# Attention with the softmax numerators of two steps in one tile: the second pair of heads of a step shares a tile with the first pair of the next

## The chip, the cores and the metric

The kernel runs on one core of one Trainium2 chip. The metric is device time in microseconds (us), the median of several runs. Engines are named as in the profile: PE is TensorE (matmuls), PEld its weight loads, ACT is ScalarE, DVE is VectorE, POOL is GpSimd, SP is SyncE, which issues most DMAs.

## The reference

One transformer block on 2048 tokens of width 448: adaptive layer norm (shift, scale and gate come from a condition `c`), attention with 16 heads of 28, a second adaptive layer norm, and an MLP of width 1792.

```python
mod = (_silu(c) @ w_mod).reshape(c.shape[0], 6, 1, -1)          # sa, ca, ga, sb, cb, gb
h = _layernorm(x) * (1 + ca) + sa
q, k, v = split(h @ wqkv)                                        # 16 heads of 28
p = softmax(q @ k.T * 28 ** -0.5)                                # per head, 2048 x 2048
x = x + ga * ((p @ v) @ wo)
h = _layernorm(x) * (1 + cb) + sb
x = x + gb * (_gelu(_layernorm(h) @ w1 + b1) @ w2 + b2)
```

All is float32. Matmuls take float32 operands as two rounded parts, a high and a low one (`hi`, `lo`), and sum three products of them.

## The kernel before

The kernel has three stages. Up to about 181 us it loads and splits weights, normalises, and computes Q, K and V; Q and K are parked in HBM by groups of four heads. From there to about 850 us it computes attention. The rest is the MLP.

**Attention** is a loop of 256 steps, 16 units of 16 steps. A unit is one group `g` of four heads and one block `qt` of 512 queries; a step takes one tile `kt` of 128 keys. The program is written in the order in which it runs, and each engine takes its instructions in that order. A step does the following.

- *Scores.* For each pair of heads (`hf` 0, then 1) PE writes a PSUM tile `s` of 128 keys x 2 heads x 512 queries: three products (hi hi, lo hi, hi lo) per head, so six matmuls of 32 rows a pair (L1046). Heads 0 and 1 use the array's rows 0 to 63, heads 2 and 3 the rows 64 to 127. `s` has two buffers, so the first pair's scores of a step wait until the first Exp of the step before has read its buffer, and the second pair's for the second Exp. From about step 236 on it has three.
- *Exp.* Behind each pair, ScalarE takes `exp(SCALE * s)` into the tile `pt` (L1051): two heads of 512 queries, 1024 elements a partition. The **first Exp** of a step is that of heads 0 and 1, the **second Exp** that of heads 2 and 3. The softmax maxima are in the scores already (they enter as an extra row of Q), and the sums come out of the product with V through a column of ones.
- *Maxima of later units.* Between the score matmuls, `emit_max` inserts three or four small jobs a step, in turns: PE computes a block of approximate scores into a PSUM tile `mx` of three buffers (L392), and VectorE reduces it to its maximum (L397). They use the half of the array that the scores beside them leave free. They last until about step 236.
- *P times V ("AV").* PE multiplies V with the Exps of the step **before** (`pend`, L1054): four matmuls, one a head, each in 32 columns of the array (L1016). In the profile each is two records, so 8 a step. They use all 128 rows of the array, so the scores of the next step stand behind them.

At a unit's end ScalarE copies the output tile `o` to `osb` (L984), and over the next steps it is divided by its sums and stored or, in the last four units (one per query block), multiplied with `wo` (steps 8 to 11 of a unit).

**Where P lies.** `pt` is a tile of four heads, 128 x 4 x 512, in one of three places of SBUF, `c0`, `c1` and `d0`, in turns (`ptags`, L1021 and L1035): a step's four heads are one tile. The profile calls them `slot_c` and `slot_d`. In stage one the places hold other data. A tile laid in a place must wait for the last that was there: for its readers (AV, on PE) and for its writers (Exps, on ScalarE). The first instruction that writes into it carries these waits. The tile framework puts them there, one semaphore per engine waited for; a wait on PE for scores and one for AV are one wait, for the later of the two. The wait for an earlier writer on ScalarE is a second one.

**An instruction and its waits.** Where an instruction needs two waits, the built program has an instruction in front of it that does nothing but wait; the profile calls it EVENT_SEMAPHORE.

Of the kernel before, what the change touches and what calls it, by code (L numbers as in the profile page):

```python
# [13 lines left out]
F32 = mybir.dt.float32  # L14
F32R = mybir.dt.float32r
AF = mybir.ActivationFunctionType
# [21 lines left out]
SCALE = float(DH) ** -0.5  # L38
# [3 lines left out]
def tile_adaln_block(ctx: ExitStack, tc: tile.TileContext, x, wqkv, wo, w1, b1, w2, b2, c, w_mod, out):  # L42
    nc = tc.nc
    pe, act, dve, pool, sp = nc.tensor, nc.scalar, nc.vector, nc.gpsimd, nc.sync
# [11 lines left out]
    def nm(t):  # L56
        uid[0] += 1
        return f"{t}_{uid[0]}"
# [4 lines left out]
    def slot(tag, shape, dt=F32R):  # L63
        return sb.tile(shape, dt, tag="slot_" + tag, name=nm("slot_" + tag), bufs=1)
# [11 lines left out]
    def ps_s2():  # L76
        return psp[0].tile([128, 2, 512], F32, tag="s", name=nm("s"), bufs=psp[2])
# [7 lines left out]
    def ps_o():  # L85
        return o_pool[0].tile([128, 512], F32, tag="o", name=nm("o"), bufs=1)
# [183 lines left out]
    d0 = slot("d0", [128, 4, 512], F32)  # L270
# [30 lines left out]
    v_sb = [sb.tile([128, 4, H, 32], F32, tag=f"slot_v{i}", name=f"v{i}", bufs=1) for i in range(4)]  # L301
# [141 lines left out]
    def tick_late(force=False):  # L443
        for e in late:
            e[0] -= 1
        while late and late[0][2] in qst and (force or late[0][0] <= 0):
            late.pop(0)[1]()
# [44 lines left out]
    def emit_max(n, half=None):  # L492
        for _ in range(n):
            if not mxq:
                return
            fits = [x for x, m in enumerate(mxq[:32]) if half is None or (m[4] // 2 == half and m[4] != last_j[0])]
            g, qt, cch, i, j = mxq.pop(fits[0] if fits else 0)
            last_j[0] = j
            max_one(g, qt, cch, i, j)
            count(g, qt, [cch])  # L500
# [27 lines left out]
    def finish_max(g, qt):  # L528
        while left[(g, qt)] > 0:
            emit_max(1)  # L530
# [42 lines left out]
    def load_k(g, ch):  # L573
        kst[(g, ch)] = load_parts(f"a{ch}", 1, g, slice(ch * 512, (ch + 1) * 512))

    def load_q(u):
        g, qt = divmod(u, NB)
        qst[u] = load_parts(f"b{u % 2}", 0, g, slice(qt * 512, (qt + 1) * 512))
# [107 lines left out]
    def share(n_mx, n_s):  # L686
        if shared:
            shared.pop().__exit__(None, None, None)
        shared.append(tc.tile_pool(name=nm("ps"), bufs=1, space=PSUM))
        psp[:] = [shared[0].__enter__(), n_mx, n_s]  # L690
# [291 lines left out]
    def end_unit(u, o):  # L982
        o_sb = sbt("osb", [128, 512], bufs=2)
        act.copy(o_sb, o)  # L984
        base = (u + 1) * NKT
        for d, fn in unit_end_tasks(u, o_sb):
            at(base + 1 + d, fn)

    pend = None
    o = None  # L990
# [14 lines left out]
    def n_maxima(s_):  # L1005
        n_plain, n_wo = left_steps(s_)
        over = len(mxq) - 7 * n_plain // 2
        if is_wo(s_):
            return max(0, -(-over // max(n_wo, 1))) if s_ % NKT > 8 else 0
        plain[0] += 1  # L1010
        return 4 if plain[0] % 2 or (over > 3 * n_wo and over > 0) else 3

    def av(u, kt, p, o):
        g = u // NB
        for j in range(4):
            pe.matmul(  # L1016
                o[32 * j : 32 * j + 32, :], v_sb[kt // 4][:, kt % 4, 4 * g + j, :], p[:, j, :],
                start=(kt == 0), stop=(kt == NKT - 1),
            )

    ptags = ["c0", "c1", "d0"]  # L1021
    done_max = set()
    for u in range(NU):
        g, qt = divmod(u, NB)
        for kt in range(NKT):
            step = u * NKT + kt
            if kt == 1 and u + 1 < NU and u + 1 not in qst:
                load_q(u + 1)
            if kt == NKT - 6 and u + 1 < NU:
                finish_max(*divmod(u + 1, NB))  # L1030
            tick_late()
            if not (three or mxq or late):
                three = True
                share(1, 3)
            pt = slot(ptags[step % 3], [128, 4, 512], F32)  # L1035
            n = n_maxima(step)
            n0 = 1 if n == 3 and step % 4 == 3 else 2

            ks, qs = kst[(g, kt // 4)], qst[u]
            kc = slice((kt % 4) * 128, (kt % 4 + 1) * 128)  # L1040
            for hf in range(2):
                s2 = ps_s2()
                for term, (kp, qp) in enumerate(((0, 0), (1, 0), (0, 1))):
                    for jj in range(2):
                        rows_ = slice(64 * hf + 32 * jj, 64 * hf + 32 * jj + 32)
                        pe.matmul(s2[:, jj, :], ks[rows_, kp, kc], qs[rows_, qp, :], start=(term == 0), stop=(term == 2))  # L1046
                    if hf == 0 and term < min(n0, n):
                        emit_max(1, 1)
                    if hf == 1 and ((term == 0 and n - n0 > 0) or (term == 2 and n - n0 > 1)):
                        emit_max(1, 0)  # L1050
                act.activation(pt[:, 2 * hf : 2 * hf + 2, :], s2, AF.Exp, scale=SCALE)  # L1051
            if pend is not None:
                pu, pkt, pp, po = pend
                av(pu, pkt, pp, po)  # L1054
                if pkt == NKT - 1:
                    end_unit(pu, po)
            if kt == 0:
                o = ps_o()
            pend = (u, kt, pt, o)
            if qt == NB - 1 and kt % 4 == 3 and g + 1 < NG:  # L1060
                load_k(g + 1, kt // 4)
            for fn in sched.pop(step, ()):
                fn()
    av(*pend)
    end_unit(pend[0], pend[3])
    tail = {}
# [87 lines left out]
```

## Time and profile before

| | us |
|---|---|
| median of 3 runs | 1149.93 |
| lowest and highest | 1149.39 and 1150.04 |
| the profiled execution, first to last instruction (its span) | 1147.0 |
| attention, first to last AV, in the profile | 185.2 to 851.8 |

The time of a run is a little longer than the span of a profiled one, since it also holds what lies before the first and behind the last instruction: 2.9 us, if the profiled execution took the median.

How the rows of the profile are read: in a timeline a row is the start, the length, engine, line of the kernel, operation, written tile <- read tiles, shapes, how many instructions were merged into it, and in brackets how long the engine was idle before it and what is thought to have ended that. In a group the figures are total busy time and the mean in ns of one. The end of a matmul is modelled, and matmuls in different rows or columns of the array run at the same time, so a busy PE may still have room. TensorE's granted clock was 1.000 over the whole span.

### The profile page before, as it was taken

What the parts mean: (1) busy time and instruction counts of PE and PEld (TensorE: products, weight loads), DVE (VectorE), ACT (ScalarE), POOL (GpSimd) and SP (SyncE); (2) the same over time, 40 slices, a digit from 0 to 9 for tenths busy, and PEclk for the clock granted to TensorE, in tenths of its full rate; (3) what the DMA queues carried; (4) which work ended last, traced back from release to release, by engine and by line L of the source; (5) the groups of instructions that cost most, each with busy time, mean ns of one, the idle gap of its engine ahead of it and who ended that gap; (6) DMA issues with size and microseconds to landing.
All of it is one profiled execution on the core that took longest, in us unless ns stands there. A gap on an engine that the chain in (4) does not pass through costs nothing.

```text
span 1147.0 us, 20808 instructions
## 1 busy us (share of the span) xinstructions
PE 1134.5 (99%) x8380; PEld 679.5 (59%) x8380; DVE 828.7 (72%) x1487; ACT 682.5 (60%) x839; POOL 216.8 (19%) x235
## 2 busy tenths in 40 slices
PE   8999999999999999999999999999999999999998
PEld 6767765444443444444444444545458888888887
DVE  6868788999998899989999977583648853444322
ACT  4656757777777877777877777675862321111110
POOL 2534432210000000000000011204514503123000
PEclk9999999999999999999999999999999999999999
DMA  9642354111132111321110222022213100000000
GB/s 299 204 148 110 107 184 130 44 60 57 45 96 66 57 39 38 94 66 57 59 55 21 83 84 62 24 84 68 68 46 95 42 33 1 1 33 1 33 1 33
DMA packets 51305, 81.09 MB, mean 71 GB/s; under 512 B 12700, under 2 KB 21760, under 8 KB 51208
## 3 DMA queue, kind: packets, MB, share of 16 engines
q1 hardware_dynamic: 50248, 78.73, 21.6%
q8 instruction: 66, 1.08, 0.4%
q0 software_dynamic: 672, 0.56, 0.2%
q10 hardware_dynamic: 288, 0.46, 0.1%
q14 instruction: 31, 0.25, 0.1%
HBM read 53.11 MB, written 26.35 MB: 69 GB/s over the span
## 4 chain that ended last, share of the span: by engine, by line
PE 96%; DVE 1%; ACT 1%; issue 1%; SPq 0%; DMA 0%; DVEq 0%; POOL 0%; POOLq 0%; ACTq 0%
PE s L1046 27%; PE o L1016 22%; PE mx L317 16%; PE pa L339 7%; PE mx L392 6%; PE s L1104 4%; PE s L1105 4%; PE s L1103 4%; PE pa L317 3%; PE pa L276 1%; PE o L240 1%; PE mx L240 1%; ACT slot_c L1051 0%; PE o L547 0%; PE pa L279 0%
## 5 line engine op out<-in xcount | busy, mean ns | idle before, releaser
L397 DVE TENSOR_REDUCE mxp<-mx 128x1 f32<-128x512 f32 x919 | 579.6, 685 | 105.9 <-PE mx L392 101.2
L1046 PE MATMUL s<-slot_b,slot_a 32*128 32x512 f32 x3072 | 383.7, 422 | 1.9 <-ACT full L814 0.7
L1051 ACT ACTIVATE slot_c<-s 128x1024 f32<-128x1024 f32 x342 | 331.6, 1022 | 83.8 <-PE s L1046 82.3
L1046 PEld LDWEIGHTS s<-slot_b,slot_a 32*128 32x128 f32 x3072 | 214.4, 183 | 254.5 <-ACT slot_c L1051 151.3
L392 PE MATMUL mx<-kh,qh 32*128 32x512 f32 x899 | 289.6, 470 | 1.2 <-DVE mxp L397 0.9
L1051 ACT ACTIVATE slot_d<-s 128x1024 f32<-128x1024 f32 x170 | 164.8, 1021 | 42.7 <-PE s L1046 42.6
L1016 PE MATMUL o<-slot_c,v 128*32 128x512 f32 x1368 | 183.1, 605 | 0.6 <-ACT osb L984 0.4
L1087 ACT ACTIVATE full<-mx,b_col 128x512 f32<-128x512 f32 x56 | 38.6, 689 | 191.8 <-PE mx L317 175.3
L392 PEld LDWEIGHTS mx<-kh,qh 32*128 32x128 f32 x899 | 116.1, 182 | 8.5 <-DVE mxp L397 5.2
L1090 DVE CAST hi<-full 128x512 fp32r<-128x512 f32 x56 | 25.2, 451 | 129.2 <-ACT full L1087 129.2
L783 POOL TENSOR_TENSOR osb<-osb,osb 128x512 f32<-128x512 f32 x16 | 20.9, 1305 | 463.4 <-DMA osb<-drec 295.1
L1016 PE MATMUL o<-slot_d,v 128*32 128x512 f32 x680 | 90.6, 605 | 0.0
L1016 PEld LDWEIGHTS o<-slot_c,v 128*32 128x32 f32 x1368 | 27.1, 108 | 57.5 <-issue 53.7
L317 PE MATMUL mx<-y,slot_a 128*128 128x512 f32 x160 | 60.6, 395 | 0.0
L405 ACT ACTIVATE slot_d<-mx 128x512 f32<-128x512 f32 x48 | 27.0, 596 | 40.1 <-PE mx L392 40.0
L1091 DVE TENSOR_TENSOR lo<-full,hi 128x512 fp32r<-128x512 f32 x56 | 44.1, 788 | 5.2
L317 PE MATMUL mx<-y,slot_c 128*128 128x512 f32 x152 | 47.5, 396 | 0.1
L1105 PE MATMUL s<-slot_v,lo 128*128 128x448 f32 x128 | 46.7, 365 | 0.0
L1103 PE MATMUL s<-slot_v,hi 128*128 128x448 f32 x128 | 46.6, 364 | 0.0
L317 PE MATMUL mx<-y,slot_v 128*128 128x512 f32 x112 | 39.2, 396 | 0.0
L317 PE MATMUL mx<-y,slot_b 128*128 128x512 f32 x112 | 39.1, 398 | 0.0
L339 PE MATMUL pa<-slot_c,slot_a 128*128 128x512 f32 x136 | 37.0, 405 | 0.0
(223 smaller groups left out, 1388.7 us busy)
## 6 DMA issues: line engine op xcount, KB each, us to landing
d<-lo SPq DMA_DIRECT2D x32, 256.0 KB
slot_b<-d SPq DMA_DIRECT2D x32, 256.0 KB
slot_a<-d SPq DMA_DIRECT2D x32, 256.0 KB
d<-hi SPq DMA_DIRECT2D x20, 256.0 KB
osb<-drec SPq DMA_DIRECT2D x14, 256.0 KB
out_dram<-xn SPq DMA_DIRECT2D x16, 224.0 KB
slot_v<-in_w_mod_dram SPq DMA_DIRECT2D x4, 784.0 KB
raw<-in_B_w_dram SPq DMA_DIRECT2D x14, 224.0 KB
```

Source lines behind the costliest of these rows:

```text
L317: pe.matmul(p, a, b, start=(i == 0), stop=(i == len(terms) - 1))
L339: pe.matmul(p, *ts[i], start=(i == 0), stop=(i == len(ts) - 1))
L392: pe.matmul(m, qh_sb[(g, qt)][js, i * 128 : (i + 1) * 128], k[js, :], start=True, stop=True)
L397: dve.tensor_reduce(out=mxp[(g, qt)][:, i, j, cch : cch + 1], in_=m, op=ALU.max, axis=AX.X)
L1016: pe.matmul(o[32 * j : 32 * j + 32, :], v_sb[kt // 4][:, kt % 4, 4 * g + j, :], p[:, j, :], start=(kt == 0), stop=(kt == NKT - 1),)
L1046: pe.matmul(s2[:, jj, :], ks[rows_, kp, kc], qs[rows_, qp, :], start=(term == 0), stop=(term == 2))
L1051: act.activation(pt[:, 2 * hf : 2 * hf + 2, :], s2, AF.Exp, scale=SCALE)
L1087: act.activation(gf, p, AF.Gelu_apprx_tanh, bias=b1_col[:, i : i + 1])
L1091: dve.tensor_tensor(out=glo, in0=gf, in1=f(ghi), op=ALU.subtract)
L1103: pe.matmul(pp, ghi[:, ts], w_hi, start=(m == 0), stop=False)
L1104: pe.matmul(pp, ghi[:, ts], w_lo, start=False, stop=False)
L1105: pe.matmul(pp, glo[:, ts], w_hi, start=False, stop=(m == NFT - 1))
```

## The change

A tile of P still holds four heads in one of the same three places, but it begins half a step later. A step's first Exp writes into the second half of the tile that the step before began (`p_next[:, 2:4, :]`); its second Exp lays a new tile and writes into its first half, and the next step's first Exp fills that one up. `pt` becomes a list of two halves, and AV reads heads 0 and 1 from one tile and heads 2 and 3 from the next. The first half of the pattern is primed by a tile laid before the loop, in `c1`.

```diff
             pe.matmul(
-                o[32 * j : 32 * j + 32, :], v_sb[kt // 4][:, kt % 4, 4 * g + j, :], p[:, j, :],
+                o[32 * j : 32 * j + 32, :], v_sb[kt // 4][:, kt % 4, 4 * g + j, :], p[j // 2][:, j % 2, :],
...
-    ptags = ["c0", "c1", "d0"]
+    p_no = [0]
+
+    def p_tile():
+        p_no[0] += 1
+        return slot(("c0", "c1", "d0")[p_no[0] % 3], [128, 4, 512], F32)
+
+    p_next = p_tile()
...
-            pt = slot(ptags[step % 3], [128, 4, 512], F32)
+            pt = [p_next[:, 2:4, :]]
...
-                act.activation(pt[:, 2 * hf : 2 * hf + 2, :], s2, AF.Exp, scale=SCALE)
+                if hf == 1:
+                    p_next = p_tile()
+                    pt.append(p_next[:, 0:2, :])
+                act.activation(pt[hf], s2, AF.Exp, scale=SCALE)
```

No instruction of an engine is added, removed or passed by another. What moves are the tiles, and with them the waits. On ScalarE, three consecutive steps of the first unit before the change (the written tile, the scores read, and the semaphores waited for; the two Exps of a step stand one below the other, and the scores `s_2324` and `s_2338` are one step's):

```order
L1051 ACTIVATE slot_c_545_2282<-s_2283 128x1024 [waits PE_49,Activation_49]
L1051 ACTIVATE slot_c_545_2282<-s_2297 128x1024 [waits PE_49]
L1051 ACTIVATE slot_d_554_2323<-s_2324 128x1024 [waits PE_49,Activation_49]
L1051 ACTIVATE slot_d_554_2323<-s_2338 128x1024 [waits PE_49]
L1051 ACTIVATE slot_c_560_2353<-s_2354 128x1024 [waits PE_49,Activation_49]
L1051 ACTIVATE slot_c_560_2353<-s_2368 128x1024 [waits PE_49]
```

The same three steps after it:

```order
L1060 ACTIVATE slot_d_545_2277<-s_2283 128x1024 [waits PE_49]
L1060 ACTIVATE slot_c_552_2310<-s_2297 128x1024 [waits PE_49,Activation_49]
L1060 ACTIVATE slot_c_552_2310<-s_2324 128x1024 [waits PE_49]
L1060 ACTIVATE slot_c_560_2348<-s_2338 128x1024 [waits PE_49,Activation_49]
L1060 ACTIVATE slot_c_560_2348<-s_2354 128x1024 [waits PE_49]
L1060 ACTIVATE slot_d_567_2381<-s_2368 128x1024 [waits PE_49,Activation_49]
```

The wait for an earlier Exp (`Activation_49`) stood at a step's first Exp and stands at its second one. Counted over the program, first Exps with two or more waits are 251 of 256 before and 2 after; second Exps with two are none before and 252 after.

On PE, the second pair of scores of a step of the same unit, an AV and the first scores behind it, before (`o` is the output, `v` is V):

```order
L1046 MATMUL s_2623<-slot_b_429_1795,slot_a_494_2048 128x512 [waits Activation_49]
L1046 MATMUL s_2623<-slot_b_429_1795,slot_a_494_2048 128x512
L392 MATMUL mx_2626<-kh_294_1276,qh_283_1235 128x512 [waits DVE_49]
L1046 MATMUL s_2623<-slot_b_429_1795,slot_a_494_2048 128x512 x4
L1016 MATMUL o_2176<-slot_c_606_2571,v_258 32x512 [waits Pool_49]
L1016 MATMUL o_2176<-slot_c_606_2571,v_258 32x512 x3
L1046 MATMUL s_2639<-slot_b_429_1795,slot_a_494_2048 128x512 [waits Activation_49]
```

And after:

```order
L1052 MATMUL s_2623<-slot_b_429_1795,slot_a_494_2048 128x512 [waits Activation_49]
L1052 MATMUL s_2623<-slot_b_429_1795,slot_a_494_2048 128x512
L392 MATMUL mx_2626<-kh_294_1276,qh_283_1235 128x512 [waits DVE_49]
L1052 MATMUL s_2623<-slot_b_429_1795,slot_a_494_2048 128x512 x4
L1016 MATMUL o_2177<-slot_c_606_2566,v_258 32x512 [waits Pool_49]
L1016 MATMUL o_2177<-slot_c_606_2566,v_258 32x512
L1016 MATMUL o_2177<-slot_d_613_2599,v_258 32x512 x2
L1052 MATMUL s_2639<-slot_b_429_1795,slot_a_494_2048 128x512 [waits Activation_49]
```

AV takes two matmuls from each of two tiles; its only wait here is the one for V, which it had before.

## The prediction

> **What bounds the kernel now.** I read the page first, for the share of each engine and the chain that ended last.
>
> ```profile
> span 1147.0 us, 20808 instructions
> PE 1134.5 (99%) x8380; PEld 679.5 (59%) x8380; DVE 828.7 (72%) x1487; ACT 682.5 (60%) x839; POOL 216.8 (19%) x235
> ...
> PE 96%; DVE 1%; ACT 1%; issue 1%; SPq 0%; DMA 0%; DVEq 0%; POOL 0%; POOLq 0%; ACTq 0%
> ```
>
> By these, TensorE is the limit and ScalarE matters nowhere. But a score matmul uses half of the array's rows, so a busy PE can still be waiting with its other half. So I asked the trace for the Exp line (L1051): its instructions, what ScalarE idled for before them (indented, us and times), and who waited for them.
>
> ```profile
> L1051 ACTq EVENT_SEMAPHORE  x251: 17/17/1592, 180.7 to 849.3; - x126
> ...
>   PE s L1046: 124.9, 245
> ...
>   PEld s L1046: 225.7, 334
> ```
>
> ScalarE waited 245 times for scores, and the weight loads of scores waited 334 times for an Exp: the two engines pass work in a ring. There is also an instruction that only waits for a semaphore, 251 times in 256 steps.
>
> Third, the timeline of two steps in the middle, per engine. The first column is the start in us, the second the length of the merged piece, the last the idle time before it. Weight loads of PE:
>
> ```profile
> 438.17 0.16 PEld L1016 LDWEIGHTS o<-slot_d,v 128*32 128x32 f32 x8 [0.29 <-issue]
> 439.17 0.18 PEld L1046 LDWEIGHTS s<-slot_b,slot_a 32*128 32x128 f32 x2 [0.84 <-ACT slot_c L1051]
> ...
> 440.33 0.16 PEld L1016 LDWEIGHTS o<-slot_c,v 128*32 128x32 f32 x8 [0.37 <-issue]
> 441.33 0.18 PEld L1046 LDWEIGHTS s<-slot_b,slot_a 32*128 32x128 f32 x2 [0.84 <-ACT slot_c L1051]
> ...
> 442.22 0.19 PEld L1046 LDWEIGHTS s<-slot_b,slot_a 32*128 32x128 f32 x2 [0.36 <-ACT slot_c L1051]
> ...
> 443.12 0.16 PEld L1016 LDWEIGHTS o<-slot_c,v 128*32 128x32 f32 x8 [0.28 <-issue]
> 444.11 0.18 PEld L1046 LDWEIGHTS s<-slot_b,slot_a 32*128 32x128 f32 x2 [0.84 <-ACT slot_d L1051]
> ...
> 445.28 0.16 PEld L1016 LDWEIGHTS o<-slot_d,v 128*32 128x32 f32 x8 [0.36 <-issue]
> ```
>
> ScalarE in the same time (x2 is the first and the second Exp of a step; one alone takes 1.02, so the second starts 0.92 after the first):
>
> ```profile
> 440.23 1.94 ACT L1051 ACTIVATE slot_c<-s 128x1024 f32<-128x1024 f32 x2 [0.85 <-PE s L1046]
> 442.40 1.94 ACT L1051 ACTIVATE slot_d<-s 128x1024 f32<-128x1024 f32 x2 [0.23 <-PE s L1046]
> ```
>
> Steps alternate: a short one (three maxima; scores at 439.17, next P times V, "AV", at 440.33) and a long one (four; 441.33 and 443.12). Follow ring A from the short step's scores: 439.17, first Exp 1.06 later at 440.23; both Exps done 1.94 later at 442.17; that frees the second score buffer, whose next weights load 0.05 later, at 442.22, in the long step; AV 0.90 later at 443.12; AV holds the array until the next short step's scores 0.99 later, at 444.11. Sum 4.94: exactly the two steps. Ring B starts at the long step's scores: 441.33, first Exp at 442.40 (1.07), both done at 444.34 (1.94), AV of the next short step at 445.28 (0.94), and scores 1.00 behind it: 4.95. So two steps take 4.95 because of a ring through ScalarE, and the wait of its first Exp for the scores lies in both rings. The 0.84 before the first scores of a step, also put down to ACT, is none of it: those loads come 0.99 to 1.00 behind AV each time, so it is AV that they wait for.
>
> How many steps run like this: windows over the AV line (8 records a step; PE and PEld busy):
>
> ```profile
> 185.18:685.65 500.47, 213.08 (x1600) 31.47 (x1600) 1.00 0.20 60
> 685.65:701.17 15.52, 4.26 (x32) 0.63 (x32) 1.00 0.00 1
> 701.17:733.73 32.56, 12.79 (x96) 1.89 (x96) 1.00 0.25 75
> 750.84:775.75 24.91, 10.65 (x80) 1.58 (x80) 1.00 0.30 97
> 799.79:820.54 20.75, 10.70 (x80) 1.62 (x80) 1.00 0.25 82
> ```
>
> 200 steps to 685.65, then 4 steps of 3.9 with the output projection's matmuls among them (other such stretches lie between the rows shown), and 12, 10 and 10 steps of the ring kind: 232 steps, 116 pairs. The last ten are shorter (two in 4.15 instead of about 5.0): no maxima are left there, and AV itself waits for the second Exp.
>
> **The change.** What an Exp computes, its length, the number of matmuls and the order of every engine stay. By the order of the program, first Exps that wait for two semaphores (the scores and an earlier Exp, the last writer of the tile) go from 251 to 2, second Exps from 0 to 252. An instruction carries one wait here, so a second wait is a separate instruction: it moves from the first Exp to the second.
>
> *What it costs at the first Exp.* The trace has the cure in it already: the tile of step 2 had no earlier Exp to wait for, so its first Exp waits for scores alone; step 3 has both. Loads of scores and of AV, then the Exps:
>
> ```profile
> 186.18 0.18 PEld L1046 LDWEIGHTS s<-slot_b,slot_a 32*128 32x128 f32 x2 [0.84 <-ACT slot_c L1051]
> ...
> 188.93 0.18 PEld L1046 LDWEIGHTS s<-slot_b,slot_a 32*128 32x128 f32 x2 [0.84 <-ACT slot_d L1051]
> ...
> 190.07 0.16 PEld L1016 LDWEIGHTS o<-slot_d,v 128*32 128x32 f32 x8 [0.37 <-issue]
> ```
>
> ```profile
> 187.19 1.94 ACT L1051 ACTIVATE slot_d<-s 128x1024 f32<-128x1024 f32 x2 [0.86 <-PE s L1046]
> 189.99 1.03 ACT L1051 ACTIVATE slot_c<-s 128x1024 f32<-128x1024 f32 x1 [0.86 <-PE s L1046]
> ```
>
> Step 2: 187.19 - 186.18 = 1.01. Step 3: 189.99 - 188.93 = 1.06, as at 440.23. The extra instruction is worth 0.05, or 0.06 with rounding: I take 0.055 a ring, though it is recorded as 17 ns. [...]
>
> *What it costs at the second Exp.* ScalarE is busy with the first one for 0.92 when it comes. Where such a pair of waits already stands behind a running instruction, it is hidden: the first Exp behind the copy at a unit's end.
>
> ```profile
> 807.75 0.59 ACT L984 COPY osb<-o 128x512 f32<-128x512 f32 x1
> 808.22 1.98 ACT L1051 ACTIVATE slot_c<-s 128x1024 f32<-128x1024 f32 x2
> ```
>
> That Exp waits for two semaphores and still starts 0.47 after a copy of 0.59, in its tail. So I cost the second Exp at 0; uncovered it would cost the same 0.055, and the gain would be gone. In a short step all scores are in long before; in a long step the second pair's last scores come late, but they come earlier by the same ring.
>
> *The rest at nothing, with cover.* AV reads two tiles. Its matmuls take 605 ns from c and from d tiles alike, and the order shows no new wait on it: heads 2 and 3 don't wait for the next step's Exp in the other half of their tile. A half is written again when the AV that read it stands a step back in PE's queue, before the scores that the Exp needs anyway. If that cover were gone, the Exp would wait up to an AV, 1.00.
>
> *Sum.* Of 116 pairs I take off three that something else sets: for example PE and VectorE stood for a DMA here.
>
> ```profile
> 350.71 0.25 DVE L774 RECIPROCAL den<-den 128x16 f32<-128x16 f32 x1 [2.39 <-DMA den<-osb]
> ```
>
> 113 x 0.055 = 6.2 us. The span goes from 1147.0 to 1140.8; 2.9 us lie outside it (1149.93 median less 1147.0), so 1143.7. Ends: 116 x 0.06 = 7.0, 1142.9; and 113 x 0.045 = 5.1, 1144.8, if the next limit takes 0.01 a pair.
>
> **Rivals.** *VectorE takes over.* Here is a long step whose AV waits for a maximum instead: loads, reductions, and the reduction's mean from the page.
>
> ```profile
> 230.94 0.18 PEld L1046 LDWEIGHTS s<-slot_b,slot_a 32*128 32x128 f32 x2 [0.84 <-ACT slot_c L1051]
> ...
> 232.26 0.18 PEld L392 LDWEIGHTS mx<-kh,qh 32*128 32x128 f32 x1
> 232.69 0.16 PEld L1016 LDWEIGHTS o<-slot_c,v 128*32 128x32 f32 x8 [0.25 <-issue]
> ```
>
> ```profile
> 231.52 2.49 DVE L397 TENSOR_REDUCE mxp<-mx 128x1 f32<-128x512 f32 x4
> ```
>
> ```profile
> L397 DVE TENSOR_REDUCE mxp<-mx 128x1 f32<-128x512 f32 x919 | 579.6, 685 | 105.9 <-PE mx L392 101.2
> ```
>
> The fourth maximum needs the buffer of the first: 231.52 + 0.69 = 232.21, its load at 232.26, AV 0.43 later. Such a long step takes 232.69 - 230.94 = 1.75 to its AV, the shortest short step 190.07 - 188.93 = 1.14, and AV twice 1.00: 4.89. That is where my ring lands (4.95 - 0.055 = 4.89), so the two tie, and every disturbance that 4.95 now swallows would count. If 0.02 a pair is lost to it, 113 x 0.035 = 4.0 remain: 1146.0. For it: VectorE's idle time is down to 0.2 to 0.3 a step. Against: the tie leaves nearly all of the gain.
>
> *No change.* Either the second Exp comes 0.055 later for its new wait, so that it ends where it ends now, or the array is full anyway: 1149.9. For it: PE's 99%. [...] Against it: rings A and B close to 0.01 through ScalarE.
>
> *Slower.* The new wait stands between two Exps that overlap by 0.10 (two in 1.94, one in 1.02). If it breaks the overlap and adds itself, the second starts 1.02 + 0.055 behind the first instead of 0.92: 0.155 later, less 0.055 at the first, 0.10 a pair, 113 x 0.10 = 11.3: 1161.2. It decides as soon as the start-to-start time of the two exceeds 0.975. Against it: the copy and Exp above overlap by 0.12 with the same two waits.
>
> **How the numbers follow.** Forecast 1143.7: 0.72 (its own range 1142.9 to 1144.8). VectorE: 0.12, 1146.0. No change: 0.10. Slower: 0.06. A range of 1142.5 to 1146.9 takes the forecast's ends and the VectorE case with about as much again for spread, and leaves out the last two. About 0.2% (2.3 us) is what a measurement of this kernel can tell from no change; both of the first cases lie beyond it: faster 0.84, same 0.10, slower 0.06.
>
> **What would show it.** In the trace after, the wait-only instruction stands between the Exps; the first Exp starts 1.00 to 1.01 behind its scores' load in nearly every step; the pair of Exps still takes 1.94; two steps take 4.89 to 4.90, and the first 200 steps about 495 instead of 500.5. Stretches with projection matmuls, and all before 181 and behind 850, stay as they are. I am wrong if the pair of Exps takes 2.0, if 1.06 stays, or if two steps stay at 4.95 while the first Exp is early: then the fourth maximum or another wait sets AV.

## The result, and the profile after

| | before | after |
|---|---|---|
| median of 7 runs each, us | 1150.04 | 1144.60 |
| lowest and highest, us | 1148.94, 1156.75 | 1143.68, 1147.34 |
| span of the profiled execution, us | 1147.0 | 1142.7 |

The ratio of after to before is 0.9949, with an interval of 0.9931 to 0.9967. Faster was forecast, with 1143.7 us and a range of 1142.5 to 1146.9; the median lies 0.9 above the forecast.

The page of the kernel after looks as before:

```profile
span 1142.7 us, 20811 instructions
PE 1130.1 (99%) x8380; PEld 678.2 (59%) x8380; DVE 827.9 (72%) x1487; ACT 683.4 (60%) x839; POOL 217.0 (19%) x235
```

PE is busy for 99% as before, and the time fell all the same. The Exp line (L1060 now), with the wait-only instruction among its rows:

```profile
L1060 ACTq EVENT_SEMAPHORE  x254: 17/17/1588, 180.6 to 845.2; - x127
...
  PE s L1052: 119.8, 242
```

There are about as many wait-only instructions as before (254, were 251). Two steps in the middle, weight loads of PE first. As before the change, a short step is followed by a long one. The loads of an AV stood in one row; where its two tiles have different names they now alternate between them, and I show the first of each:

```profile
433.10 0.18 PEld L1052 LDWEIGHTS s<-slot_b,slot_a 32*128 32x128 f32 x2 [0.84 <-ACT slot_d L1060]
...
434.25 0.11 PEld L1016 LDWEIGHTS o<-slot_d,v 128*32 128x32 f32 x2 [0.37 <-issue]
...
435.24 0.18 PEld L1052 LDWEIGHTS s<-slot_b,slot_a 32*128 32x128 f32 x2 [0.84 <-ACT slot_c L1060]
...
436.10 0.18 PEld L1052 LDWEIGHTS s<-slot_b,slot_a 32*128 32x128 f32 x2 [0.32 <-ACT slot_c L1060]
...
437.00 0.16 PEld L1016 LDWEIGHTS o<-slot_c,v 128*32 128x32 f32 x8 [0.25 <-issue]
437.99 0.18 PEld L1052 LDWEIGHTS s<-slot_b,slot_a 32*128 32x128 f32 x2 [0.84 <-ACT slot_c L1060]
...
439.13 0.11 PEld L1016 LDWEIGHTS o<-slot_c,v 128*32 128x32 f32 x2 [0.36 <-issue]
```

The Exps of the same time:

```profile
434.11 1.94 ACT L1060 ACTIVATE slot_c<-s 128x1024 f32<-128x1024 f32 x2 [0.81 <-PE s L1052]
436.25 1.03 ACT L1060 ACTIVATE slot_c<-s 128x1024 f32<-128x1024 f32 x1 [0.20 <-PE s L1052]
437.17 1.02 ACT L1060 ACTIVATE slot_d<-s 128x1024 f32<-128x1024 f32 x1
439.00 1.03 ACT L1060 ACTIVATE slot_d<-s 128x1024 f32<-128x1024 f32 x1 [0.81 <-PE s L1052]
```

Ring A now reads: scores 433.10, first Exp 1.01 later (was 1.06), both Exps 1.94, the second score buffer loaded 0.05 behind them, AV 0.90, next scores 0.99: 4.89. Ring B: 435.24, 1.01, 1.94, AV at 439.13 (0.94 behind 438.19). One term has changed, the first one. Over steps 3 to 199 the median distance from the load of the scores to the first Exp went from 1066 to 1007 ns, the two Exps of a step start 921 ns apart (920 before), and the median of two steps fell from 4951 to 4890 ns.

**Where the gain is, and where it isn't.** I cut the first 200 steps at the load of AV of steps 0, 64, 72, 128, 136 and 200 and asked for the AV line in each stretch (8 records a step; PE and PEld busy, PEclk, the share of the DMA engines, GB/s). Before:

```profile
185.18:344.26 159.08, 68.19 (x512) 10.07 (x512) 1.00 0.20 59
344.26:365.81 21.55, 8.52 (x64) 1.26 (x64) 1.00 0.22 73
365.81:504.67 138.86, 59.66 (x448) 8.82 (x448) 1.00 0.20 60
504.67:524.83 20.16, 8.52 (x64) 1.26 (x64) 1.00 0.13 47
524.83:685.65 160.82, 68.19 (x512) 10.07 (x512) 1.00 0.20 61
```

After:

```profile
185.16:342.16 157.00, 68.19 (x512) 10.07 (x512) 1.00 0.20 59
342.16:365.36 23.20, 9.39 (x64) 1.30 (x64) 0.93 0.20 69
365.36:502.75 137.39, 59.67 (x448) 8.81 (x448) 1.00 0.20 59
502.75:523.46 20.71, 8.53 (x64) 1.26 (x64) 1.00 0.16 54
523.46:682.48 159.02, 68.19 (x512) 10.07 (x512) 1.00 0.20 61
```

The three long stretches are 184 steps, 92 pairs. They became shorter by 2.08, 1.47 and 1.80: 5.35, which is 0.058 a pair. The two short stretches, 8 steps each, became longer by 1.65 and 0.55. In each of them the division at a unit's end stands in VectorE's queue:

```profile
348.83 0.25 DVE L774 RECIPROCAL den<-den 128x16 f32<-128x16 f32 x1 [2.60 <-DMA den<-osb]
...
508.48 0.25 DVE L774 RECIPROCAL den<-den 128x16 f32<-128x16 f32 x1 [1.67 <-DMA den<-osb]
```

The reciprocal waits 2.60 for the DMA that brings the sums (2.39 before), the reductions of the maxima stand behind it in VectorE's order, and PE, which stood for 0.86 us here before the change, stands for 1.13. In the second stretch the same wait went from 0.7 to 1.7. So 2.2 us of the gain were lost here in this execution. The first stretch shows more than that wait explains: its granted clock is 0.93. In steps of 3 us (busy time of PE, PEld, DVE, ACT and POOL, then PEclk):

```profile
346.00:349.00 3.00, 2.55 (x25) 1.01 (x25) 0.40 (x3) 2.05 (x3) 0.00 (x0) 1.00 0.06 10
349.00:352.00 3.00, 2.24 (x15) 0.97 (x15) 3.00 (x7) 1.16 (x2) 0.00 (x0) 0.95 0.05 7
352.00:355.00 3.00, 3.00 (x21) 1.16 (x23) 1.47 (x4) 0.78 (x1) 0.00 (x0) 0.50 0.22 83
```

Behind the standstill TensorE ran at half its clock for 3.41 us, and its AV matmuls took 9.39 in this stretch instead of 8.52. In the trace before, the clock stayed at 1.00 behind the standstill at this place.

### The profile page after: what moved, and what is told of

The parts are those of the page before. It is cut to its first block, busy times and chain, and to the rows that moved or that the text cites. A ratio compares the mean times of both kernels' runs of the same rounds, so it can differ in the third digit from the quotient of the medians.

```text
span 1142.7 us, 20811 instructions
## 1 busy us (share of the span) xinstructions
PE 1130.1 (99%) x8380; PEld 678.2 (59%) x8380; DVE 827.9 (72%) x1487; ACT 683.4 (60%) x839; POOL 217.0 (19%) x235
## 4 chain that ended last, share of the span: by engine, by line
PE 92%; DVE 2%; DMA 2%; ACT 1%; POOL 1%; issue 1%; SPq 0%; DVEq 0%; ACTq 0%; POOLq 0%
PE s L1052 25%; PE o L1016 21%; PE mx L317 16%; PE pa L339 7%; PE mx L392 7%; PE s L1113 4%; PE s L1114 4%; PE s L1112 4%; PE pa L317 3%; PE o L240 1%; DMA slot_c<-in_w_mod_dram 1%; PE mx L240 1%; DMA den<-osb 1%; POOL xn L849 0%; POOL xn L848 0%
## 5 line engine op out<-in xcount | busy, mean ns | idle before, releaser
L1060 ACT ACTIVATE slot_c<-s 128x1024 f32<-128x1024 f32 x341 | 339.6, 1022 | 82.2 <-PE s L1052 81.8
L1052 PE MATMUL s<-slot_b,slot_a 32*128 32x512 f32 x3072 | 377.9, 421 | 1.6 <-ACT full L814 0.7
L392 PE MATMUL mx<-kh,qh 32*128 32x512 f32 x899 | 292.6, 470 | 1.7 <-DVE mxp L397 1.3
L1016 PE MATMUL o<-slot_c,v 128*32 128x512 f32 x1364 | 271.4, 606 | 0.5 <-ACT osb L984 0.4
L1060 ACT ACTIVATE slot_d<-s 128x1024 f32<-128x1024 f32 x171 | 174.7, 1022 | 38.7 <-PE s L1052 38.0
L1016 PE MATMUL o<-slot_d,v 128*32 128x512 f32 x684 | 180.8, 607 | 0.0
L1016 PEld LDWEIGHTS o<-slot_c,v 128*32 128x32 f32 x1364 | 38.1, 108 | 54.9 <-issue 50.1
L1016 PEld LDWEIGHTS o<-slot_d,v 128*32 128x32 f32 x684 | 24.7, 108 | 27.5 <-issue 25.2
```

The costliest lines, as they stand in the source:

```text
L392: pe.matmul(m, qh_sb[(g, qt)][js, i * 128 : (i + 1) * 128], k[js, :], start=True, stop=True)
L1016: pe.matmul(o[32 * j : 32 * j + 32, :], v_sb[kt // 4][:, kt % 4, 4 * g + j, :], p[j // 2][:, j % 2, :], start=(kt == 0), stop=(kt == NKT - 1),
L1060: act.activation(pt[hf], s2, AF.Exp, scale=SCALE)
```

## The experiments

The question was first whether the gain comes from the place of the wait or from the new layout, and then where the lost 2 us went. Where the text compares times at equal clock, it takes the executions of a kernel whose granted clock was 0.999 or 1.000 on average over the span.

**Halves exchanged.** The layout of before with the pairs in the other halves of a tile. The waits stay at the first Exp.

```diff
-                ... p[:, j, :],
+                ... p[:, (j + 2) % 4, :],
-                act.activation(pt[:, 2 * hf : 2 * hf + 2, :], s2, AF.Exp, scale=SCALE)
+                act.activation(pt[:, 2 - 2 * hf : 4 - 2 * hf, :], s2, AF.Exp, scale=SCALE)
```

> The kernel before with the two halves of each P tile exchanged: the first Exp of a step writes heads 0 and 1 into the second half of the tile, the second Exp into the first half, and P times V reads them there. Waits are as before (two at the first Exp, one at the second); the places in which the halves lie are those of the change. Wait theory (the gain is the second wait that leaves the first Exp): as before, ratio 1.000 within 0.002, first Exp 1.06 us behind its scores' weight load, two steps in 4.95 us. Layout theory (the gain is where the halves lie in SBUF while ScalarE writes and PE reads): about as after the change, ratio 0.995, two steps in 4.89.

Measured: 1151.02 us, ratio 0.9997 (0.9986 to 1.0008), two steps 4.95. Where the first pair lies in its tile does not matter.

**Tiles laid once.** Three tiles for the whole attention in place of one per step. Then both Exps of a step carry two waits.

```diff
-    ptags = ["c0", "c1", "d0"]
+    p_all = [slot(tag, [128, 4, 512], F32) for tag in ("c0", "c1", "d0")]
...
-            pt = slot(ptags[step % 3], [128, 4, 512], F32)
+            pt = p_all[step % 3]
```

> The kernel before with three P tiles that are laid once before the loop and written again and again, so that BOTH Exps of a step wait for an earlier Exp as well as for scores. Wait theory: the first Exp keeps its second wait, so the gain doesn't come, and the added one at the second Exp is hidden behind the first: ratio 1.000 within 0.002, 1.06 us from load to first Exp, 0.92 from first to second Exp, two steps in 4.95. If a second wait at the second Exp costs what it costs at the first (0.055 us a step there, and the second Exp lies in both rings): two steps in 5.00, about 1156 us. If the laying of a tile at each step were the cost: faster than before, about 1144.

```profile
L1051 ACTq EVENT_SEMAPHORE  x500: 17/17/1587, 181.2 to 853.3; - x167
```

Measured: 1151.73 us, ratio 0.9999 (0.9989 to 1.0009). There are 249 more wait-only instructions, and nothing changes: the second Exps start 920 ns behind the first ones, the first Exps 1066 ns behind their scores' load. A wait at the second Exp is free, alone or together with the other; a wait at the first Exp is what must go.

**The new layout, with a wait put back at the first Exp.** The layout of after, but a tile is laid a step earlier, and GpSimd writes one column of its second half (0.0, overwritten by the Exp). The first Exp then waits for GpSimd besides the scores.

```diff
+    def p_lay():
+        t = p_tile()
+        pool.memset(t[:, 2, 0:1], 0.0)
+        return t
...
-                    p_next = p_tile()
+                    p_next = p_laid
...
+            if step < NU * NKT - 1:
+                p_laid = p_lay()
```

> The changed kernel with a second wait put back at the first Exp by other means: each P tile is laid a step earlier, and GpSimd writes a zero into the first column of head 2's place in it, which the first Exp of a later step overwrites, so that this Exp waits for scores and for GpSimd (long done); the second Exp keeps its two waits. The tiles lie as after the change. Wait theory: the gain is undone, 1150 us, ratio to before 1.000 within 0.003, 1.06 us from load to first Exp, two steps in 4.95. Layout theory: the gain stays, about 1144.5, 1.01 and 4.89.

In the timeline, the load of scores and the Exp that follows it:

```profile
439.54 0.18 PEld L1058 LDWEIGHTS s<-slot_b,slot_a 32*128 32x128 f32 x2 [0.84 <-ACT slot_c L1066]
```

```profile
440.61 1.02 ACT L1066 ACTIVATE slot_d<-s 128x1024 f32<-128x1024 f32 x1 [0.81 <-PE s L1058]
```

Measured: 1149.55 us, ratio 0.9987 (0.9976 to 0.9998). The first Exp is back at 1.07, two steps at 4.95 (median 4950 ns), with the new layout in place. At equal clock this kernel takes 1149.40 (9 executions) and the kernel before, on the same chip, 1150.08 (11): the gain is undone but for 0.7 us, of which the cause is open.

**A third semaphore.** The same, and VectorE writes a second column, so that the first Exp waits for three engines.

```diff
         pool.memset(t[:, 2, 0:1], 0.0)
+        dve.memset(t[:, 3, 0:1], 0.0)
```

> As the kernel with GpSimd's column, and VectorE writes a column of head 3's place too, so that the first Exp waits for three semaphores (scores, GpSimd, VectorE): two instructions that only wait. VectorE gets 256 more short instructions. Wait theory, if each of them costs the same: 1.11 to 1.12 us from load to first Exp, two steps in 5.00, about 6 us more than before: 1156, ratio 1.005. If a second one is free, since it is passed while the first waits: 1.06, 4.95, 1150. Layout theory: 1144.5, or a little more for VectorE's instructions.

```profile
L1067 ACTq EVENT_SEMAPHORE  x509: 17/38/3714, 180.5 to 852.9; - x170
```

Measured: 1150.76 us, ratio 0.9987 (0.9972 to 1.0002). It was meant as a double dose and is none, so the 1156 of the first theory did not come. The kernel with two waits had 509 wait-only instructions as well, and in this trace 254 of the 509 wait on two semaphores, VectorE's and that of the matmuls. The first Exp comes 1056 ns behind its scores' load, not later than with two waits, and two steps take 4.94. The dose could not be varied in this way.

**The later reciprocal.** Kernel after, with the reciprocal two steps behind the DMA that it reads instead of one, and the two splits behind it one step later.

```diff
-        tasks = [(0, t_den), (1, t_rec), (4, t_split), (5, t_split2)]
+        tasks = [(0, t_den), (2, t_rec), (5, t_split), (6, t_split2)]
```

> The changed kernel with a unit's reciprocal (VectorE) two steps behind the DMA that brings its sums instead of one, the product and the split by GpSimd and VectorE one step later each. In the profiled execution after the change VectorE stood 8.1 us for that DMA in three places, 7.3 before it. Theory that these standstills ate the missing part of the gain and that PE waits for them: they go, the span falls by 3 to 6 us against the changed kernel: 1139 to 1142, ratio to before 0.991 to 0.993. Rival: the standstills are covered by other work, or come back at the next DMA (the broadcast of the reciprocals, then waited for by GpSimd and VectorE): 1144.6, ratio 0.995.

The windows over the same steps as above, the two short stretches:

```profile
342.11:361.98 19.87, 8.52 (x64) 1.26 (x64) 1.00 0.25 80
...
499.40:519.00 19.60, 8.52 (x64) 1.26 (x64) 1.00 0.18 64
```

Measured: 1141.54 us, ratio to before 0.9916 (0.9898 to 0.9933). Eight steps of the ring are 4 x 4.89 = 19.56, and both stretches now stand near that, 0.31 and 0.04 above it: the two lost 3.64 and 1.15 in the kernel after (23.20 and 20.71), and 1.75 and 0.36 before, against 4 x 4.95 = 19.80. Two steps are as long as in after (4892 ns).

**The later reciprocal alone.** The same edit of `tasks` in the kernel before.

> The kernel before with the same later reciprocal and no other change. Theory: the standstills go here too, 1150 becomes 1144.5 to 1147; and the step from here to the changed kernel with the later reciprocal is the pure effect of the wait, 115 pairs of steps by 0.058 us = 6.7 us. Rival (the standstills are covered): 1150, ratio 1.000.

Measured: 1148.71 us, ratio to before 0.9975 (0.9964 to 0.9987). Two steps stay at 4950 ns. This gain is smaller than the theory's 1144.5 to 1147: the standstills cost the kernel before some 2 to 3 us (2.1 at equal clock). The two kernels with the later reciprocal differ by 0.9916 / 0.9975 = 0.9941, 6.8 us (some 4 to 9, by the two intervals' halves, 0.0018 and 0.0012, added as squares). The kernel after with it ran at the higher clock more often; at equal clock the two take 1141.29 (4 executions) and 1147.34 (6), 6.05 apart. So 6 to 7 us are the change alone, without the standstills.

**The old layout, and the wait taken off the first Exp in another way.** Kernel before, with one small ScalarE instruction a step, ahead of the first Exp. It writes one column of the tile's second half (overwritten by the second Exp) and is the first to write into the tile.

```diff
             pt = slot(ptags[step % 3], [128, 4, 512], F32)
+            act.activation(pt[:, 2, 0:1], zero_col, AF.Exp)
```

Six rows of ScalarE's order show that the second wait has gone to the second Exp; the small instruction (L1036) has none left. In the trace of this run all 256 second Exps have a wait-only instruction in front of them, and 2 of the first ones:

```
402 L1036 ACTIVATE slot_c_1009_4479<-cst_70 128x1
403 L1052 ACTIVATE slot_c_1009_4479<-s_4481 128x1024 [waits PE_49]
404 L1052 ACTIVATE slot_c_1009_4479<-s_4495 128x1024 [waits PE_49,Activation_49]
405 L1036 ACTIVATE slot_c_1018_4518<-cst_70 128x1
406 L1052 ACTIVATE slot_c_1018_4518<-s_4520 128x1024 [waits PE_49]
407 L1052 ACTIVATE slot_c_1018_4518<-s_4531 128x1024 [waits PE_49,Activation_49]
```

> The kernel before with its old layout (a tile holds both pairs of one step), and one more ScalarE instruction per step: between the second Exp of a step and the first of the next it writes one column (exp of 0) of the new tile's second half, which the second Exp then overwrites. It is the first to write into the tile, so it takes over the dependence on the earlier Exps; the first Exp then waits for its scores alone, and the second one for scores and ScalarE. Nothing else moves. Theory (the wait-only instruction of the first Exp carries the wait for the scores, and the Exp follows 0.045 us behind it): first Exp 1.01 behind its scores' load, two steps 4.89, the first 200 steps shorter by 5 to 6 us, time ratio to before 0.994 to 0.997, with 256 instructions more on ScalarE. Rival (the new layout itself saves something, or the tile half a step later): no gain, 1.000. Rival (what counts is ScalarE's number of instructions in the ring): the small write takes about 0.2 out of an idle time of 0.23, and where it doesn't fit the time is longer than before, 1.002 or more.

Loads of scores and ScalarE's row for the step:

```profile
442.12 0.18 PEld L1047 LDWEIGHTS s<-slot_b,slot_a 32*128 32x128 f32 x2 [0.84 <-ACT slot_c L1052]
```

```profile
440.97 1.94 ACT L1052 ACTIVATE slot_c<-s 128x1024 f32<-128x1024 f32 x2 [0.71 <-PE s L1047]
442.80 0.20 ACT L1036 ACTIVATE slot_d<-cst 128x1 f32<-128x1 f32 x1
443.13 1.02 ACT L1052 ACTIVATE slot_d<-s 128x1024 f32<-128x1024 f32 x1
```

Measured: 1146.22 us, ratio 0.9955 (0.9939 to 0.9971); at equal clock 1143.99 (3 executions), against 1149.88 for before (5). The small write runs from 442.80 to 443.00 in time that ScalarE would have idled, and the first Exp starts 1.01 behind its load (443.13 - 442.12), median 1006 ns. Two steps take 4890 ns, as with the new layout. The first 200 steps took 497.8 in the profiled execution, 2.7 less than before where 5 to 6 was expected; 3.41 us of them were at half clock, and the second short stretch took 20.66, much as in the kernel after (20.71). So the layout is only a carrier: what counts is that the first Exp has one wait.

**The same with the later reciprocal.** Both edits in the kernel before.

> The same, with the reciprocal two steps behind its DMA instead of one, and the two splits one step later. Theory: it loses nothing at the reciprocals, as the changed kernel with the later reciprocal did: ratio to before 0.991 to 0.994, two steps 4.89. If the small writes cost ScalarE something: 0.995 to 0.998, and then two steps 4.90 to 4.93. If the layout is needed: 0.9975, as the kernel before with the later reciprocal alone.

Measured: 1141.43 us (1141.36 to 1141.59), ratio 0.9911 (0.9898 to 0.9925), level with the kernel after with the later reciprocal. These two are the fastest of the study.

At equal clock, in us, with the number of executions (the kernel before ran beside each group):

| kernel | first Exp waits | median | before beside it |
|---|---|---|---|
| after | once | 1144.19 (4) | - |
| halves exchanged | twice | 1150.70 (9) | 1150.08 (11) |
| tiles laid once | twice | 1149.04 (2) | 1150.08 (11) |
| wait put back | twice | 1149.40 (9) | 1150.08 (11) |
| third semaphore | three times | 1149.08 (4) | 1150.08 (11) |
| old layout, small write | once | 1143.99 (3) | 1149.88 (5) |
| before, later reciprocal | twice | 1147.34 (6) | 1149.45 (7) |
| after, later reciprocal | once | 1141.29 (4) | 1149.45 (7) |
| old layout, small write, later reciprocal | once | 1141.43 (4) | 1149.88 (5) |

## Why the prediction was right, step by step

*The ring sets the time, not the busy PE.* Right. Only the term "scores to first Exp" changed, and the two steps followed it: 59 ns less there (1066 to 1007), 61 ns less in the pair (4951 to 4890). Judged by the busy share alone, with PE at 99% and ScalarE at 60%, the time would have stayed as it was; the 99% stayed, and the kernel became 5.4 us shorter.

*The wait is worth 0.055.* Right, and a little low: 0.058 a pair in the undisturbed stretches. Why it costs that much although it is recorded as 17 ns can be read in the records of single instructions. Times in ns from the start of the span, before and after:

```
before  EVENT_SEMAPHORE  440171 to 440188   first Exp starts 440232
after   (no such instruction ahead of it)    first Exp starts 438998
```

Over some 190 first Exps of each trace, the median from the modelled end of the last score matmul to the Exp is 97 ns before and 38 after. Before, the wait-only instruction ends 52 ns behind the scores, and the Exp starts 44 or 45 ns behind that in every one of them. So it is the wait-only instruction that waits for the scores; the Exp itself is left with the semaphore that was satisfied long ago, and comes as a second instruction in a row. The trace names the semaphores and bears this out. In the kernel before, all 251 wait-only instructions wait on semaphore 109, the one on which the 256 second Exps wait for their scores, and the 251 Exps behind them wait on 106, which the Exps raise themselves. So the wait that comes last stands in front, in the extra instruction. What the other order would cost was not run, and no run shows what the 59 ns between 97 and 38 consist of.

*The second Exp's wait is free.* Right: 921 ns from first to second Exp, 920 before, and 249 more of these waits changed nothing with the tiles laid once. There is little to spare, though. In 30 of the 98 long steps from 3 to 199 in the trace after, the second Exp starts less than 50 ns behind the end of its own wait-only instruction, and up to 932 ns behind the first Exp: the second pair's scores come so late there that the wait is only just covered.

*Layout and AV at nothing.* Right: an exchange of halves does nothing, the new layout with a wait put back gains next to nothing, and the old layout without the wait gains all.

*The sum.* Its main term held, and its edges did not. 113 x 0.055 = 6.2 was forecast for the span, and 4.3 came in the profiled execution; the first 200 steps took 497.3 (682.48 - 185.16) where about 495 was named. Three pairs were taken off for standstills, as if those would stay as long as they were. They grew: from the issue of the transfer to the reciprocal it is 1.90 and 1.96 us in the two stretches, before and after alike, while the steps ahead became shorter, so VectorE comes earlier and waits longer. Of the 2.2 us lost, 0.55 are in the second stretch. In the first, the wait grew by only 0.21, and much of the 1.65 is the half clock: the kernel with the wait put back stood there as long (2.67 for the DMA, PE for 1.14) at full clock, and lost 2.50 against its ring (22.30 for the 8 steps), where the kernel after lost 3.64. By these two, an estimate of 1.1 is the clock's, which the prediction could not foresee. With the reciprocal two steps behind its DMA, the change is worth 6.05 at equal clock and 6.8 by the ratios.

The forecast of 1143.7 also took 2.9 us as lying outside the span, the distance of a median from another execution's span. Now each run has both numbers: 1144.60 and 1142.7 for the profiled execution after, 1.8 us as the median over its seven. The rest of the 2.9 is that the profiled execution before was a short one: with a span of 1147.0 it lies below all nine executions of the kernel before at a clock of 1.000 in the first group of experiments (1147.2 to 1148.6). Executions at a lower clock are longer still (there: 1150.08 at a clock of 0.999 and over, 1152.68 at 0.997 and 0.998). The two slips go in opposite directions, 1.9 us too much gain and 1.0 us too much outside. So it is in part luck that the median came out only 0.9 from the forecast.

The projection stretch stayed as forecast, 15.46 after 15.52:

```profile
682.49:697.95 15.46, 4.26 (x32) 0.63 (x33) 1.00 0.01 1
```

*The rivals.* VectorE took nothing: this rival left 0.035 of the gain in a pair, and the undisturbed stretches show 0.058. The long step to its AV takes 1.76 (435.24 to 437.00) against the 1.75 of the prediction's step whose AV waits for a maximum: the two limits are about equal now, and a further gain in the ring may end there. "No change" fell with the ring, "slower" with the 921 ns.

## What to carry to other kernels

Where two engines hand work back and forth, look at the order for the waits of the instruction that ends the ring's idle time. Here the second semaphore of the first Exp cost a second instruction (251 in 256 steps), the one that waited last was the extra one, and the Exp came 59 ns later for it. Let another instruction be first to write into a recycled tile, one that stands behind running work or in idle time (a new cut of the tile, or a write of one column). Then look at what the faster loop reaches earlier: here a transfer took the same 1.90 us from its issue to the reciprocal before and after, PE stood for 1.13 us behind it instead of 0.86, and it took part of the gain back until its reader was moved behind it (1144.19 to 1141.29 us at equal clock).

## What the runs showed of the hardware

TensorE's clock fell to half behind short standstills, in some executions and not in others. In the trace after it was 0.50 from 351.7 to 355.1 us, behind a standstill of PE of 1.13 us. With the third semaphore it did so too, behind 1.09. With the wait put back at the first Exp, PE stood for 1.14 at the same place and the clock stayed at 1.00. At the start of attention PE stands for 0.62 in all ten traces, and four of them show the half clock behind it; here the kernel before with the later reciprocal (columns as above):

```profile
183.00:186.00 3.00, 2.72 (x20) 1.50 (x23) 3.00 (x6) 2.32 (x3) 0.00 (x0) 0.64 0.90 260
186.00:189.00 3.00, 3.00 (x20) 1.16 (x23) 0.52 (x2) 1.02 (x1) 1.99 (x3) 0.50 0.10 27
189.00:192.00 3.00, 3.00 (x31) 1.27 (x27) 2.24 (x5) 1.94 (x2) 1.10 (x2) 0.72 0.33 74
```

In the traces before and after these 9 us are at 1.00. The half clock lasted 3.41 us in the trace after, and 6.83 in the one above; what sets these lengths is not shown. Whether a standstill sets it off was not tried by itself; the kernels with the later reciprocal, whose PE has no standstill near 350 us, show no half clock there.
